# One product per query tile with the block maxima, ahead of the products with neighbouring keys

## The chip, the cores and the metric

One core of a Trainium2 chip runs the whole program in one launch. The metric is device time in microseconds, the median over runs. Engines are named as the profile names them: PE is TensorE's matmul stream, PEld its weight loads (one instruction stream issues both), DVE is VectorE, ACT is ScalarE, POOL is GpSimd, SP issues most DMAs.

## What is computed

Attention over 4 batches, 8 heads, 768 positions and 64 features per head, then a feed-forward layer. Each query sees two kinds of keys: the neighbouring positions (fewer than 16 away) and 24 block keys, each the maximum of 32 keys in a row, feature by feature. One softmax runs over both.

```python
k_sum = k.reshape(B, H, nb, block, D).max(axis=3)          # block 32: nb = 24
v_sum = v.reshape(B, H, nb, block, D).mean(axis=3)
scores_l = scale * np.matmul(q, k.transpose(0, 1, 3, 2))   # kept where |i - j| < 16
scores_s = scale * np.einsum('bhsd,bhnd->bhsn', q, k_sum) + np.log(block)
a = softmax(concatenate([masked scores_l, scores_s], axis=-1))
attn = np.matmul(a, concatenate([v, v_sum], axis=2))
h = x @ w_in                                               # x: attn as 3072 x 512
out = (h - np.tanh(h)) @ w_out                             # 512 -> 2048 -> 512
```

## The kernel before

The 3072 rows are cut into 8 units `u` of 384 rows (`U`): half a batch each. A unit has 4 head pairs `p`; a head pair has two heads (`a`), and its 384 queries make three query tiles (`i`, `NT = 3`) of 128 rows, each of two halves of 64. The features of head 0 lie on partitions 0 to 63 and those of head 1 on partitions 64 to 127.

`scores` (L1000) makes all scores of one head pair as one task on PE; there are 8 x 4 = 32 such tasks, called score blocks here. For each tile the task first multiplies with the 24 block maxima of `top` (far products), then with the at most 94 neighbouring keys of each half (near products; 79 at an end of the sequence). Head `a` writes its own PSUM bank, `ss[a]`: `pS` and a second one (`pY0`, later `pT`). Half 0 goes to partitions 0 to 63 of the bank, half 1 to partitions 64 to 127. Queries are the stationary operand (64 features x 64 queries), keys move. All operands are 32-bit floats, and the profile shows two weight loads and two matmuls for each product (called passes here): 24 products, 48 passes in a block. In units 0 and 1 queries and keys come from `qf` and `kT` (tiles `q`, `kT`), in units 2 to 7 from `rawq0` and `raw` (tiles `rawq`, `raw`).

Behind a block comes `softmax` (L1023): DVE takes the sum with a mask and its minimum for each tile and head, ACT the exponential, DVE the sums and the scaling. Then the probabilities are turned (`p turn`: on PE in units 0 and 1, by DVE and DMA later) and `values` multiplies them with `v`. Between these small tasks PE runs the feed-forward products (`pH` banks for the first layer, `pY` and others for the second).

Nothing is scheduled at run time. Each task is put on record by `do(kind, engine, cost, ...)`; `Plan.follow` (L337) emits all tasks in the order of a table written out by hand (`ORDER`) and uses the stated costs only to place up to some dozens of idle products (`keep_warm`, L1538: `ident` by `ident` into `pX`) in modelled gaps of the first 100 us. The `scores` task has a stated cost of 1.07 us before and after. `k turn` (L983, transposes of keys on PE) and `sum` (L878, block sums of `v`) are other PE tasks that are named below.

Of the kernel before, what the change touches and what calls it, by code (L numbers as in the profile page):

```python
# [535 lines left out]
def program(  # L536
# [12 lines left out]
    tensor, vector, scalar, gpsimd, sync = engines.values()  # L549
    B, H, S, D = q.shape  # L550
    DM, F = w_in.shape[0], w_in.shape[1]
    P = 128
    U = S // 2
    NT = U // P
# [3 lines left out]
    NB = S // 32  # L558
# [4 lines left out]
    WIN = 15  # L563
    NK = 64 + 2 * WIN
    N2 = NB + NK
# [20 lines left out]
    def do(kind, engine, cost, go, r=(), w=(), before=()):  # L586
        plan.add(kind, {engine: cost}, go, r, w, before)
# [16 lines left out]
    def bank(base, tag):  # L604
        plan.banks.add(base)
        if tag == "pX":
            made_by[base] = lambda: px_bank
            plan.ring(tag, 1, base)
            return base
        return buf(base, tag, [P, 512], bufs=2 if tag == "pH" else 1, pool=pp)  # L610

    def at(base):
        if base not in made:
            made[base] = made_by[base]()
        return made[base]
# [374 lines left out]
    def tops(b, p):  # L990
        base = ("top", b, p // PG)
        if base not in made_by:
            buf(base, f"top{p // PG}", [P, PG * NB])
        return base, p % PG
# [5 lines left out]
    def scores(u, p, tags):  # L1000
        ss, b, t0 = [bank(("s", u, p, a), tags[a]) for a in range(2)], u // 2, U * (u % 2)
        top, m = tops(b, p)
        if u < WHOLE:
            q_all, k_all = lambda: at(("qf",))[:, p % 2], lambda: at(("kT",))[:, p]
            r = [(("qf",), p % 2)] + [(x, n) for x, n in [(("kT",), (p, 0)), (("kT",), (p, 1)), (top, (m, 0)), (top, (m, 1))]]
        else:
            (q_all, qr), (k_all, kr) = block_q[u, p], block_k[b, p]
            r = [*qr, *kr, (top, m)]

        def go():  # L1010
            for i in range(NT):
                for near in range(2):
                    for a in range(2):
                        for half in range(2):
                            rows, x = slice(64 * a, 64 * a + 64), P * i + 64 * half
                            first = t0 + x - WIN
                            lo, hi = max(first, 0), min(first + NK, S)
                            w = k_all()[rows, lo:hi] if near else at(top)[rows, NB * m:NB * (m + 1)]
                            c = N2 * i + (NB + lo - first if near else 0)
                            tensor.matmul(at(ss[a])[64 * half:64 * half + 64, c:c + (hi - lo if near else NB)], q_all()[rows, x:x + 64], w, start=True, stop=True)  # L1020
        do("scores", PE, 1.07, go, r=r, w=[(s, 0) for s in ss])

    def softmax(u, p):  # L1023
# [402 lines left out]
    def moe_slot(m):  # L1426
        if PAIRS and FIRST <= m < NM:
            kk, n = divmod(m - FIRST, 4)
            pair, k = divmod(kk, HALF_F)
            return PAIRS[pair][n in (1, 2)], 2 * k + (n > 1)  # L1430
        return divmod(m, NF) if 0 <= m < NM else None

    def moe_at(j):

        return j if not PAIRS or j < FIRST else -1 if j < FIRST + GAP else j - GAP
# [12 lines left out]
    for j in range(NS + LAG + 3 + (GAP if PAIRS else 0)):  # L1448
        m, m1, m2 = (moe_slot(moe_at(j - LAG - n)) for n in range(3))
        early = j < NP * SLOTS  # L1450
        s0 = slot(j)
        if s0 is not None:
            u, p, i = s0
# [46 lines left out]
        if s0 is not None and not early:  # L1500
            u, p, i = s0
# [78 lines left out]
```

## Time and profile before

| | |
|---|---|
| median of 3 runs | 643.25 us (643.18 to 645.22) |
| the profiled execution | 641.7 us |
| its span, first to last instruction | 640.0 us |
| PE busy | 624.0 us, 97% |
| PEld busy | 532.0 us, 83% |
| DVE, ACT, POOL busy | 486.6, 422.6, 172.5 us |
| mean granted clock of PE | 0.995 |

The span is the profiled execution less 1.7 us around it. Durations in the profile come from that one execution. A matmul's record includes the time that its result takes to come through the array, so records of consecutive matmuls overlap, and a busy share of PE near 100% doesn't by itself say that it is fed without pause; distances between starts do. `64*128 64x24` in a row says that the stationary operand has 64 partitions and 128 columns and that 24 columns move.

### The profile page before, as it was taken

What the parts mean: (1) busy time and instruction counts of PE and PEld (TensorE: products, weight loads), DVE (VectorE), ACT (ScalarE), POOL (GpSimd) and SP (SyncE); (2) the same over time, 40 slices, a digit from 0 to 9 for tenths busy, and PEclk for the clock granted to TensorE, in tenths of its full rate; (3) what the DMA queues carried; (4) which work ended last, traced back from release to release, by engine and by line L of the source; (5) the groups of instructions that cost most, each with busy time, mean ns of one, the idle gap of its engine ahead of it and who ended that gap; (6) DMA issues with size and microseconds to landing.
All of it is one profiled execution on the core that took longest, in us unless ns stands there. A gap on an engine that the chain in (4) does not pass through costs nothing.

```text
span 640.0 us, 14660 instructions
## 1 busy us (share of the span) xinstructions
PE 624.0 (97%) x5163; PEld 532.0 (83%) x5163; DVE 486.6 (76%) x1349; ACT 422.6 (66%) x1270; POOL 172.5 (27%) x191
## 2 busy tenths in 40 slices
PE   6989999999999999999999999999999999999996
PEld 5877666688888888888888889988898889989995
DVE  3989999998797787567785788685659878677662
ACT  3979788678767777656767556555557754554545
POOL 2130003134313331130313104235351043315330
PEclk9989999999999999999999999999999999999998
DMA  8867886856687787877875641000000100000002
GB/s 297 199 197 225 226 231 191 182 116 185 162 165 161 186 228 167 186 174 160 236 198 165 192 132 55 0 2 1 0 2 1 65 35 1 1 1 1 2 0 102
DMA packets 159765, 77.27 MB, mean 121 GB/s; under 512 B 121704, under 2 KB 148552, under 8 KB 159688
## 3 DMA queue, kind: packets, MB, share of 16 engines
q1 hardware_dynamic: 159416, 76.09, 46.0%
q8 instruction: 42, 0.69, 0.5%
q14 instruction: 35, 0.29, 0.1%
q10 hardware_dynamic: 272, 0.20, 0.1%
HBM read 58.12 MB, written 17.84 MB: 119 GB/s over the span
## 4 chain that ended last, share of the span: by engine, by line
PE 85%; DVE 6%; DMA 4%; ACT 2%; SPq 1%; issue 1%; POOL 1%; DVEq 0%; POOLq 0%; ACTq 0%
PE pH L233 37%; PE pY L233 30%; PE pS L233 6%; PE pT L233 6%; PE pX L233 6%; DVE raw L233 2%; DMA raw<-in_moe_w_out_dram 1%; DVE tmp L233 1%; DVE prob L233 1%; SPq L233 1%; DMA xl<-in_k_dram 1%; DMA tmp<-in_v_dram 1%; DMA raw<-in_moe_w_in_dram 1%; DVE wf L233 1%; POOL xf L233 1%
## 5 line engine op out<-in xcount | busy, mean ns | idle before, releaser
L233 PE MATMUL pH<-xh,w 128*128 128x384 f32 x608 | 155.9, 346 | 0.0
L233 PE MATMUL pY<-wf,gh 128*128 128x512 f32 x321 | 133.9, 454 | 0.2 <-DVE gh L233 0.2
L233 ACT ACTIVATE prob<-prob,stats 128x118 f32<-128x118 f32 x298 | 109.4, 385 | 35.3 <-DVE stats L233 33.7
L233 PEld LDWEIGHTS pH<-xh,w 128*128 128x128 f32 x608 | 109.0, 188 | 9.2 <-issue 3.1
L233 POOL TENSOR_TENSOR gl<-gu,gh 128x384 fp32r<-128x384 f32 x45 | 46.9, 1041 | 134.1 <-ACT gh L233 71.7
L233 POOL TENSOR_TENSOR gu<-gu,gt 128x384 f32<-128x384 f32 x49 | 51.3, 1048 | 105.8 <-ACT gu L233 60.5
L233 PEld LDWEIGHTS pY<-wf,gh 128*128 128x128 f32 x321 | 59.4, 188 | 19.4 <-issue 10.8
L233 ACT ACTIVATE gu<-gu 128x384 f32<-128x384 f32 x128 | 65.7, 517 | 1.1
L233 ACT ACTIVATE gh<-gu 128x384 fp32r<-128x384 f32 x71 | 36.8, 520 | 42.3 <-PE pY L233 16.7
L233 PE MATMUL pH<-xl,w 128*128 128x384 f32 x192 | 64.6, 336 | 0.0
L233 ACT ACTIVATE gu<-tmp 128x384 f32<-128x384 f32 x64 | 33.2, 518 | 37.2 <-DVE gl L233 19.4
L233 DVE TENSOR_TENSOR gl<-gu,gh 128x384 fp32r<-128x384 f32 x67 | 41.1, 613 | 13.0 <-ACT gh L233 9.3
L233 DVE TENSOR_TENSOR gu<-gu,gt 128x384 f32<-128x384 f32 x63 | 35.5, 567 | 8.7 <-ACT gu L233 8.5
L233 ACT ACTIVATE gt<-pH 128x384 f32<-128x384 f32 x64 | 30.7, 482 | 15.8 <-PE pH L233 15.6
L233 ACT ACTIVATE gu<-pH 128x384 f32<-128x384 f32 x64 | 30.9, 482 | 14.3 <-PE pH L233 9.4
L233 ACT ACTIVATE gt<-tmp 128x384 f32<-128x384 f32 x64 | 32.4, 512 | 11.9 <-DVE tmp L233 7.9
L233 ACT ACTIVATION_READ_ACCUMULATOR prob<-prob,stats 128x1 f32 x192 | 36.6, 190 | 0.0
L233 PE MATMUL pY<-kT,gh 128*128 128x512 f32 x90 | 36.5, 406 | 0.0
L233 PEld LDWEIGHTS pH<-xl,w 128*128 128x128 f32 x192 | 36.0, 187 | 0.0
L233 PE MATMUL pY<-kT,gl 128*128 128x512 f32 x90 | 35.4, 394 | 0.0
L233 POOL TENSOR_TENSOR xf<-xf 128x256 f32<-128x256 f32 x25 | 19.5, 781 | 56.1 <-DVE xf L233 55.0
L233 DVE CUSTOM_DVE_ANT_0 prob<-pS,mask 128x118 f32<-128x118 f32 x96 | 25.6, 275 | 11.6 <-PE pT L233 10.2
(306 smaller groups left out, 1627.9 us busy)
## 6 DMA issues: line engine op xcount, KB each, us to landing
place<-turned SPq DMA_DIRECT2D x96, 96.0 KB
probT<-place SPq DMA_DIRECT2D x24, 384.0 KB
raw<-in_moe_w_in_dram SPq DMA_DIRECT2D x16, 512.0 KB
raw<-in_moe_w_out_dram SPq DMA_DIRECT2D x16, 512.0 KB
vw<-in_v_dram SPq DMA_DIRECT2D x80, 96.0 KB
rawq<-in_q_dram SPq DMA_DIRECT2D x96, 48.0 KB
tmp<-in_v_dram SPq DMA_DIRECT2D x24, 192.0 KB
raw<-in_k_dram SPq DMA_DIRECT2D x48, 96.0 KB
```

The lines of the kernel that those rows point to most:

```text
L233: return lambda *args, **kwargs: self._tc.keep_in_program_order(op(*args, **kwargs))
```

## The change

In `scores` the far products come out of the tile loop: a first loop over the three tiles and two heads makes one far product each, with all 128 queries of the tile as stationary operand, and writes both halves of the bank at once. The near products follow in a loop of their own, in the order in which they stood before. A block has 6 far and 12 near products after the change in place of 12 and 12. The task's reads, writes, stated cost and place in the order stay.

```diff
         def go():
             for i in range(NT):
-                for near in range(2):
-                    for a in range(2):
-                        for half in range(2):
-                            rows, x = slice(64 * a, 64 * a + 64), P * i + 64 * half
-                            first = t0 + x - WIN
-                            lo, hi = max(first, 0), min(first + NK, S)
-                            w = k_all()[rows, lo:hi] if near else at(top)[rows, NB * m:NB * (m + 1)]
-                            c = N2 * i + (NB + lo - first if near else 0)
-                            tensor.matmul(at(ss[a])[64 * half:64 * half + 64, c:c + (hi - lo if near else NB)], q_all()[rows, x:x + 64], w, start=True, stop=True)
+                for a in range(2):
+                    rows = slice(64 * a, 64 * a + 64)
+                    tensor.matmul(at(ss[a])[:, N2 * i:N2 * i + NB], q_all()[rows, P * i:P * i + P], at(top)[rows, NB * m:NB * (m + 1)], start=True, stop=True)
+            for i in range(NT):
+                for a in range(2):
+                    for half in range(2):
+                        rows, x = slice(64 * a, 64 * a + 64), P * i + 64 * half
+                        first = t0 + x - WIN
+                        lo, hi = max(first, 0), min(first + NK, S)
+                        c = N2 * i + NB + lo - first
+                        tensor.matmul(at(ss[a])[64 * half:64 * half + 64, c:c + hi - lo], q_all()[rows, x:x + 64], k_all()[rows, lo:hi], start=True, stop=True)
         do("scores", PE, 1.07, go, r=r, w=[(s, 0) for s in ss])
```

## Rows read from the trace of the kernel before

**Rows 1.** The page: busy us of each engine, share of the span, instructions.

```profile
PE 624.0 (97%) x5163; PEld 532.0 (83%) x5163; DVE 486.6 (76%) x1349; ACT 422.6 (66%) x1270; POOL 172.5 (27%) x191
```

**Rows 2.** A group of matmuls by shape: far products; busy us, mean ns.

```profile
L233 PE MATMUL pS<-top,rawq 64*64 64x24 f32 x288 | 19.6, 206 | 0.4 <-DVE rawq L233 0.4
```

**Rows 3.** Stretch 125 to 347: length, busy PE, PEld, DVE, ACT, POOL, granted clock, DMA.

```profile
125.00:347.00 222.00, 221.44 (x2509) 191.44 (x2509) 170.96 (x617) 156.05 (x568) 59.36 (x59) 1.00 0.74 176
```

**Rows 4.** Waits of PE: us in total, times, longest us.

```profile
PE pT L233 <- DVE prob L233: 1.6, 1, 1.6
...
PE pS L233 <- DVE rawq L233: 0.4, 1, 0.4
```

**Rows 5.** Timeline of weight loads, one score block: start us, duration us.

```profile
143.12 0.14 PEld L233 LDWEIGHTS pS<-top,rawq 64*64 64x64 f32 x2 [0.25 <-issue]
143.14 0.14 PEld L233 LDWEIGHTS pT<-top,rawq 64*64 64x64 f32 x2
143.18 0.14 PEld L233 LDWEIGHTS pS<-top,rawq 64*64 64x64 f32 x2
...
143.23 0.14 PEld L233 LDWEIGHTS pS<-raw,rawq 64*64 64x64 f32 x2
...
144.12 0.19 PEld L233 LDWEIGHTS pY<-kT,gh 128*128 128x128 f32 x1
144.23 0.19 PEld L233 LDWEIGHTS pY<-wl,gh 128*128 128x128 f32 x1
```

**Rows 6.** Timeline of matmuls in the same block.

```profile
143.43 0.18 PE L233 MATMUL pS<-top,rawq 64*64 64x24 f32 x1
...
143.63 0.24 PE L233 MATMUL pS<-raw,rawq 64*64 64x94 f32 x1
...
143.71 0.18 PE L233 MATMUL pS<-top,rawq 64*64 64x24 f32 x1
...
143.95 0.24 PE L233 MATMUL pT<-raw,rawq 64*64 64x94 f32 x1
```

**Rows 7.** Timeline of weight loads of a `p turn` (transposes, 64 partitions, 118 columns).

```profile
63.67 0.13 PEld L233 LDWEIGHTS pT<-ident,prob 64*118 64x118 f32 x1 [0.76 <-ACT gt L233]
63.67 0.13 PEld L233 LDWEIGHTS pS<-ident,prob 64*118 64x118 f32 x1
63.73 0.14 PEld L233 LDWEIGHTS pT<-ident,prob 64*118 64x118 f32 x1
```

**Rows 8.** Groups of weight loads by shape: busy us, mean ns of one.

```profile
L233 PEld LDWEIGHTS pH<-xh,w 128*128 128x128 f32 x608 | 109.0, 188 | 9.2 <-issue 3.1 <-ACT gu L233 0.3 <-ACT w L233 0.2
...
L233 PEld LDWEIGHTS pT<-top,rawq 64*64 64x64 f32 x288 | 15.8, 132 | 0.2 <-DVE qa L233 0.2
...
L233 PEld LDWEIGHTS pT<-probT,vw 118*64 118x64 f32 x288 | 9.4, 137 | 4.2 <-issue 3.1 <-PE pY L233 1.1
```

**Rows 9.** Instructions of the tile `probT`, PE: ns min/median/max, first and last start.

```profile
L233 PE MATMUL pY<-probT,vw x48: 222/222/271, 31.0 to 45.0; 118*64 118x64 f32 x48
```

**Rows 10.** Timeline of matmuls: the end of `values` and what follows.

```profile
31.48 0.46 PE L233 MATMUL pY<-probT,vw 118*64 118x64 f32 x10
31.87 0.38 PE L233 MATMUL pX<-ident 128*128 128x128 f32 x1
```

**Rows 11.** Timeline of matmuls inside a `k turn` (transposes).

```profile
30.53 0.23 PE L233 MATMUL pT<-ident,xl 64*128 64x64 f32 x1
30.54 0.27 PE L233 MATMUL pH<-ident,xl 64*64 64x64 f32 x2
```

**Rows 12.** Timeline of matmuls: the starts of the third and the fourth block.

```profile
27.94 0.24 PE L233 MATMUL pS<-top,q 64*64 64x24 f32 x2
...
32.66 0.24 PE L233 MATMUL pS<-top,q 64*64 64x24 f32 x2
```

**Rows 13.** The chain that ended last, 28 to 38 us: start us, us, what.

```profile
30.56 3.68 DMA raw<-in_moe_w_out_dram
...
37.72 0.24 PE pT L233
```

## The prediction

> **What bounds the kernel.** I read the page first: PE is busy for 97% of the span [rows 1]. Then one long stretch. A block has 12 far passes in each bank, so the 288 that bank `pS` shows from `rawq` are 24 of the 32 blocks [rows 2], those of units 2 to 7; they lie between 125 and 347 us, where PE is busy for 221.44 of 222.00 us at a granted clock of 1.00, the 2.4 GHz level [rows 3]. Records of matmuls overlap, so I looked third at the waits: of those that PE has behind score blocks the longest are 1.6 and 0.4 us [rows 4]. PE sets the time: what a block gains or loses on PE, the kernel gains or loses, but for such waits. Last I took one block apart by its starts [rows 5, 6].
>
> A block holds PE from its first weight load at 143.12 to the first load of the next product at 144.12 [rows 5]: 1.00 us, 32 us in all 32 blocks. Four chains run side by side in it, one for each bank and partition half: at 143.12 and 143.14 four loads start, two for each bank. Within a chain a load of 64 columns follows the other after 0.055 us (143.12, 143.18, 143.23), so four loads take the time of one. A near pass is longer than that: from its start at 143.63 to the far pass behind it at 143.71 it streams for 0.08 us [rows 6]. By its 24 columns against 94 a far pass streams for 0.02. One tile is 0.28 us (143.43 to 143.71), and that adds up: two near streams of 0.08, and two loads of nearly 0.06 that nothing hides, those of the second far pass and the first near pass, since only 0.02 of streaming stands ahead of each. The loads of the second near pass and of the next tile's first far pass lie under near streams.
>
> So the block is 3 x 0.055 for the first two far loads and the first near load, 0.16 for its two near streams, 2 x 0.28 for two more tiles, 0.01 by which bank `pT` runs behind, and 0.09 from the last near stream's end (start 143.95, plus 0.08) to the next load at 144.12. That is 0.985, against 1.00 measured.
>
> **What the change does to it.** *Removed:* 6 of 24 products, 12 of 48 passes. They streamed for 0.02 each in four chains, and half of their loads lay under near streams.
>
> *Added:* columns. A far product now loads all 128 queries of a tile. Two chains are left, one for each bank, with 3 products of 2 passes each: 6 loads of 128 columns in a row. The trace before has no load of 64 partitions x 128 columns outside transposes, so I bound it from both sides. Low: in a `p turn` loads of 64 x 118 follow each other after 0.06 us [rows 7], but these are transposes. High: behind the block two loads of 128 x 128 start 0.11 apart, at 144.12 and 144.23, before anything streams [rows 5]. The groups choose between them: 128 x 128 takes 188 ns, 64 x 64 132 ns and 118 x 64 137 ns [rows 8], so outside transposes the columns decide and not the partitions. I take 0.11: 0.66 until the last far pass streams. Both banks' loads can go together, as they do in the `p turn` (63.67 and 63.67 [rows 7]); if they could not, the far part would take twice as long.
>
> *Moved:* the far products ahead of all near ones. Their loads lose their cover: before, one in two lay under a near stream; now each meets only the 0.02 of another far pass. And inside the block the stationary shape changes from 64 x 128 to 64 x 64. Where only the columns of the shape change outside transposes, at the end of `values`, a pause stands: the last record ends at 31.94 (31.48 plus 0.46), records of this shape last 222 ns [rows 9], so it started at 31.72, streamed its 64 columns for 0.05 and was through at 31.77; the next load starts at 31.87 [rows 10], 0.10 later, as at the end of the block (0.09). Against it speaks the `k turn`, where 64 x 128 gives way to 64 x 64 within 0.01 us [rows 11]. Bounds: 0, and 0.11, which is 0.09 and the far stream of 0.02 under which the near load could else lie. I take 0.11, since the `k turn` consists of transposes alone. The Trainium skill (TensorEngine Tiling, Key Properties) says that a change of tiling mode drains the engine: by that rule the block takes 1.405, without it 1.295. The trace agrees at `values` and not at the `k turn`.
>
> *The new block:* 0.66 for far loads, 0.02 the last far stream, 0.09 the change of shape, 0.055 the first near load, 6 x 0.08 for near streams whose other loads are hidden, 0.01 and 0.09 at the end: 1.405. Against 1.00 measured that is 0.405 more, against the 0.985 of the same reckoning 0.42. I take 0.41.
>
> *Nothing else moves.* The task keeps its reads, writes, place and cost, so no wait and no DMA is added or put behind another one, and the idle products stay as they are. Its consumer, the minimum on DVE, waits for the whole task before and after, so `softmax` starts 0.41 later, and so does all that stands behind the block on PE. What DVE and ACT have to do (486.6 and 422.6 us [rows 1]) stays.
>
> *The sum:* 32 x 0.41 = 13.1 us. Cover: the third and fourth block, at 27.94 and 32.66 [rows 12], lie beside a chain that comes from a weight DMA of 3.68 us at 30.56 through DVE to PE at 37.72 [rows 13], where PE waited 1.6 us [rows 4]; their 0.8 us are hidden there. The wait of 0.4 us, for a query tile that no block feeds, is eaten up by the blocks ahead of it. If that cover is gone, 1.2 us come back. I expect a span of 640.0 + 11.9 = 651.9 and a profiled execution of 653.6 against 641.7. The median of the runs shown, 643.25, lies 1.55 above the profiled execution; added to the median the sum gives 655.2.
>
> **Rivals.**
> 1. *No pause at the change of shape.* As in the `k turn` [rows 11] the first near load lies under the last far stream: 0.41 - 0.11 = 0.30 a block, 9.6 us, less 1.2 of cover: 651.7. For it: that one group. Against it: the end of `values` [rows 10].
> 2. *Loads as fast as in transposes.* At 0.06 each the far part is 0.36 in place of 0.66 [rows 7]: 0.11 a block, 3.5 us, less some 0.6: 646.2. If the pause is missing too, nothing is left of it: 643.3, no change. Against it: the groups of loads [rows 8].
> 3. *Passes set the pace, and the kernel gets faster.* If a block's 1.00 us were the price of 48 passes, 0.0208 each, 12 fewer would save 0.25 us, and 32 blocks 8.0 us: 635.3. It decides from the point where the distance between issued passes, and not a chain's own load, spaces the starts. Against it: four loads start within some 0.02 us, and then each chain waits until 0.055 is over [rows 5]. A rule that points this way stands in the Trainium skill (TensorEngine Tiling, Instruction Overhead): a matmul costs about 60 cycles however few columns move. My estimate from that page at 2.4 GHz is 25 ns for each of 12 passes, 9.6 us in 32 blocks, 633.7. The trace disagrees: starts lie less than 0.02 apart in the block.
> 4. *The two banks' loads take turns.* 12 x 0.11 in place of 6 x 0.11: 1.07 a block, 34.2 us less 1.2 of cover, 676. Against it: the `p turn` [rows 7].
>
> **How the numbers follow.** The forecast, 0.41 a block, has 0.66; no pause 0.15; fast loads 0.06, and with no pause too 0.03; faster by passes 0.06; loads in turns 0.04. A change of 0.3%, 1.9 us, is about what a measurement of this kernel can tell from none. Faster has 0.06, the same 0.03, slower 0.91. The range reaches from 650.0, below the case without a pause, to 658.0, which is 0.46 a block with nothing hidden; forecast and first rival hold 0.81 together. The forecast's own range is 653 to 658.
>
> **What would show it.** In the trace after: half as many weight loads from `top`, of the shape 64 x 128 and 188 ns long, 0.11 apart in each bank; 0.11 between the last far matmul's start and the first near load; blocks of 1.41 us; the same work of the stretch 125 to 347 us taking some 9 to 10 us more, still without long waits of PE. Loads 0.06 apart would show the second rival, a near load right behind the last far matmul's start the first, blocks below 1.00 us the third. The prediction is wrong if a block's length and the span don't go together, for PE would then have had slack that its waits don't show.

## The result and the profile after

The changed kernel takes 652.65 us (652.02 to 653.95) against 643.21 us (643.10 to 645.22) of the kernel before beside it: a ratio of 1.0142, 95% interval 1.0115 to 1.0168. It is slower. Run once more beside other runs of before, the ratio was 1.0183, 1.0155 to 1.0212 (654.25 us; the last experiment below). The profiled execution took 652.1 us with a span of 650.3, against 641.7 and 640.0.

The page after: busy time of each engine, which answers to [rows 1], and the chain of work that ended last, by engine:

```profile
PE 635.6 (98%) x4779; PEld 543.3 (84%) x4779; DVE 488.6 (75%) x1349; ACT 422.4 (65%) x1270; POOL 172.1 (26%) x191
...
PE 92%; DVE 4%; ACT 1%; DMA 1%; POOL 1%; issue 0%; SPq 0%; DVEq 0%; POOLq 0%; ACTq 0%
```

PE has 384 passes fewer (5163 to 4779: 12 in each of 32 blocks) and is busy for 11.6 us more. DVE and ACT have the same instructions and the same busy time within 2 us. The chain is PE nearly throughout. Now one block, the same as in [rows 5] and [rows 6], which stands 1.71 us later in this execution. First its weight loads:

```profile
144.83 0.18 PEld L233 LDWEIGHTS pS<-top,rawq 64*128 64x128 f32 x1 [0.24 <-issue]
144.84 0.18 PEld L233 LDWEIGHTS pT<-top,rawq 64*128 64x128 f32 x1
144.94 0.19 PEld L233 LDWEIGHTS pS<-top,rawq 64*128 64x128 f32 x1
...
145.38 0.19 PEld L233 LDWEIGHTS pS<-top,rawq 64*128 64x128 f32 x1
...
145.61 0.14 PEld L233 LDWEIGHTS pS<-raw,rawq 64*64 64x64 f32 x2
...
146.26 0.19 PEld L233 LDWEIGHTS pY<-kT,gh 128*128 128x128 f32 x1
```

Then its matmuls:

```profile
145.41 0.27 PE L233 MATMUL pS<-top,rawq 64*128 64x24 f32 x1
...
145.62 0.30 PE L233 MATMUL pS<-raw,rawq 64*64 64x79 f32 x2
...
146.09 0.24 PE L233 MATMUL pT<-raw,rawq 64*64 64x94 f32 x1
```

What to see: the loads of 64 x 128 are 0.11 apart in each bank (144.83, 144.94; five distances make 0.55, to 145.38), and the two banks load at the same time, 0.01 apart. At that distance the last of them is through at 145.49 and its 24 columns, 0.02 of streaming, at 145.51; the first near load starts at 145.61: a pause of 0.10. The near part takes 0.48 from there to the last matmul's start, and the next product's load follows at 146.26. The block lasts 1.43 us in place of 1.00. All 24 blocks of units 2 to 7 last 1.42 to 1.43; a group of loads by shape shows the price of one, which answers to the 132 ns in [rows 8]:

```profile
L233 PEld LDWEIGHTS pS<-top,rawq 64*128 64x128 f32 x144 | 17.8, 187 | 8.5 <-issue 6.8 <-PE pY L233 1.1 <-DVE prob L233 0.6
```

Last the stretch from the start of the ninth block to the end of the 32nd, in both kernels (length, busy PE, PEld, DVE, ACT, POOL, granted clock, DMA share, GB/s). Before:

```profile
134.75:345.64 210.89, 210.32 (x2460) 182.76 (x2460) 160.15 (x592) 149.78 (x552) 57.73 (x57) 1.00 0.75 178
```

After:

```profile
136.09:356.22 220.13, 220.13 (x2172) 191.83 (x2171) 162.04 (x592) 150.21 (x553) 57.55 (x58) 1.00 0.72 171
```

The same work takes 9.24 us more; 24 blocks are longer by 10.37 (0.432 each). The missing 1.1 us lie nearly all at one place, the block that waits for its query tile in the kernel before [rows 4]. Its lines there (weight loads, then the matmul that waits):

```profile
320.80 0.20 PEld L233 LDWEIGHTS pS<-top,rawq 64*64 64x64 f32 x4 [0.84 <-DVE rawq L233]
321.25 0.14 PEld L233 LDWEIGHTS pT<-top,rawq 64*64 64x64 f32 x2 [0.25 <-DVE qa L233]
...
322.22 0.30 PEld L233 LDWEIGHTS pH<-xh,w 128*128 128x128 f32 x2
```

```profile
320.81 0.30 PE L233 MATMUL pS<-top,rawq 64*64 64x24 f32 x4 [0.42 <-DVE rawq L233]
```

PE waited 0.42 ahead of this block, and then bank `pT` could start only at 321.25, 0.45 behind `pS`, so that the block lasted 1.42 in place of 0.99. Only 0.14 of this counts as idle time of PE, since the records of the other bank cover the rest. In the changed kernel both are gone, and the same block lasts 1.42 with its wide loads: from the start of the block ahead of it to the start of the block behind it the changed kernel takes 0.22 us less than before, though two longer blocks, 0.86, lie in between.

### The profile page after: what moved, and what is told of

Same layout as the page of the kernel before. It is cut to its first block, busy times and chain, and to the rows that moved or that the text cites. A ratio compares the mean times of both kernels' runs of the same rounds, so it can differ in the third digit from the quotient of the medians.

```text
span 650.3 us, 13892 instructions
## 1 busy us (share of the span) xinstructions
PE 635.6 (98%) x4779; PEld 543.3 (84%) x4779; DVE 488.6 (75%) x1349; ACT 422.4 (65%) x1270; POOL 172.1 (26%) x191
## 4 chain that ended last, share of the span: by engine, by line
PE 92%; DVE 4%; ACT 1%; DMA 1%; POOL 1%; issue 0%; SPq 0%; DVEq 0%; POOLq 0%; ACTq 0%
PE pH L233 39%; PE pY L233 33%; PE pS L233 9%; PE pX L233 6%; PE pT L233 6%; DVE prob L233 1%; DMA xl<-in_k_dram 1%; ACT prob L233 1%; DVE raw L233 1%; POOL xf L233 0%; DVE tmp L233 0%; DMA out_dram<-xf 0%; DVE top L233 0%; DVE vw L233 0%; DVE vsum L233 0%
```

## The experiments

**The order alone.** Far products ahead of the near ones, but with 64 queries each as before:

```diff
+            for i in range(NT):
+                for a in range(2):
+                    for half in range(2):
+                        rows, x = slice(64 * a, 64 * a + 64), P * i + 64 * half
+                        tensor.matmul(at(ss[a])[64 * half:64 * half + 64, N2 * i:N2 * i + NB], q_all()[rows, x:x + 64], at(top)[rows, NB * m:NB * (m + 1)], start=True, stop=True)
             for i in range(NT):
...
```

> The order alone: all 12 far products of 64 queries stand ahead of all near ones, nothing is merged, and the stationary shape stays 64 x 64 through the block. My theory (the loss comes from wider loads and one change of shape, not from the order): six far loads of 0.055 us, the first near load 0.055, six near streams of 0.08, 0.01 and 0.09 at the end make 0.965 by the reckoning that gave 0.985 for the kernel before, so a block stays within 0.03 of 0.99 to 1.00 and the time within 1 us of 643.2. Rival (the far loads lose the near streams as their cover, and that is the loss): half of the far passes lose some 0.05 each in four chains, a block of 1.15 and about 646 us.

Measured: 641.22 us against 642.96, 0.9966 (0.9943 to 0.9989). Weight loads of the same block:

```profile
146.43 0.14 PEld L233 LDWEIGHTS pS<-top,rawq 64*64 64x64 f32 x2 [0.36 <-issue]
...
146.48 0.14 PEld L233 LDWEIGHTS pS<-top,rawq 64*64 64x64 f32 x2
...
146.77 0.14 PEld L233 LDWEIGHTS pS<-raw,rawq 64*64 64x64 f32 x2
...
147.42 0.19 PEld L233 LDWEIGHTS pY<-kT,gh 128*128 128x128 f32 x1
```

The block is as long as before, 0.99 us: six far loads and a near one follow each other, the near one 0.34 behind the first (146.43 to 146.77), and the other near loads lie under near streams. Losing the near streams as a cover costs nothing, because in the old order as many loads stood open. The first near load follows the last far one at the usual distance, so passing from far to near products makes no pause as long as the shape stays. The rival falls. The time came out lower than the block explains, so the kernel was run again:

> The kernel of e1 once more, in more rounds: it came out at 0.9966 [0.9943, 0.9989] of before though its score blocks have the length of before. Theory (the length of a block decides, the order inside it nothing): within 0.3% of before, the interval includes 1. Rival (far products ahead help, by a way not seen): again 0.995 to 0.998, the interval below 1.

Measured: 642.19 us against 642.22, 1.0001 (0.9976 to 1.0027). The order makes no difference that can be seen; the interval of the first comparison, which left out 1, did not hold up.

**The merge alone.** The wide far products in the tile loop, so that the stationary shape changes five times in a block:

```diff
             for i in range(NT):
+                for a in range(2):
+                    rows = slice(64 * a, 64 * a + 64)
+                    tensor.matmul(at(ss[a])[:, N2 * i:N2 * i + NB], q_all()[rows, P * i:P * i + P], at(top)[rows, NB * m:NB * (m + 1)], start=True, stop=True)
...
```

> The merge alone: a far product of 128 queries for each tile and head, left in the tile loop, so that the stationary shape changes five times inside a block and not once. My theory (each change of shape empties PE, 0.09 us from the last stream to the next load): a tile takes 0.22 for two wide loads, 0.02 stream, 0.09 pause, 0.055 load, 0.16 near streams, 0.09 pause; three make a block of 1.9 us, 0.9 more than before, 29 us in 32 blocks, less some 3 of cover: about 669 us. Rival (no pause; loads lie under streams of the other shape): a tile of some 0.36, a block of 1.1 to 1.2 us, 646 to 649 us.

Measured: 669.25 us, one execution, where the theory put it. Its loads, one of each kind:

```profile
148.73 0.18 PEld L233 LDWEIGHTS pS<-top,rawq 64*128 64x128 f32 x1 [0.25 <-issue]
...
149.07 0.14 PEld L233 LDWEIGHTS pS<-raw,rawq 64*64 64x64 f32 x2
...
149.39 0.18 PEld L233 LDWEIGHTS pS<-top,rawq 64*128 64x128 f32 x1
...
150.70 0.19 PEld L233 LDWEIGHTS pY<-kT,gh 128*128 128x128 f32 x1
```

A tile takes 0.66 (148.73 to 149.39), a block 1.97. Against the changed kernel that is 0.54 for four more changes of shape, 0.135 each: the pause of 0.10, and loads behind it that nothing covers. The rival, without a pause, falls. The Trainium skill (TensorEngine Tiling, Key Properties) says that a changed tiling mode drains the engine. The trace agrees in both directions of the change: 0.10 from the last far stream to the first near load, and some 0.09 from the last near stream to the next tile's wide load.

**One change of shape and a third of the wide loads.** Only the first tile's far products are merged, all stand ahead:

```diff
+            for a in range(2):
+                rows = slice(64 * a, 64 * a + 64)
+                tensor.matmul(at(ss[a])[:, :NB], q_all()[rows, :P], at(top)[rows, NB * m:NB * (m + 1)], start=True, stop=True)
+            for i in range(1, NT):
+                for a in range(2):
+                    for half in range(2):
...
```

> One change of shape as in the changed kernel, but a third of its wide loads: the first tile's far products have 128 queries, those of the other two tiles 64, all ahead of the near ones. Theory (two causes that add up: 0.055 more for each wide load, 0.11 for the change of shape): 0.22 wide loads, 0.02 stream, 0.09 pause, 4 x 0.055 for the narrow far loads, 0.055 the first near load, 0.48 near streams, 0.10 at the end: a block of 1.19 to 1.21 us. Rival A (wide loads alone make the loss of 0.43): 1.14 us. Rival B (the change of shape alone): 1.42 us. The time is read with less care: 32 x 0.2 = 6 over before, less cover, 646 to 649 us.

Measured: 650.38 us, one execution; its loads:

```profile
151.13 0.18 PEld L233 LDWEIGHTS pS<-top,rawq 64*128 64x128 f32 x1 [0.36 <-issue]
...
151.24 0.19 PEld L233 LDWEIGHTS pS<-top,rawq 64*128 64x128 f32 x1
...
151.47 0.14 PEld L233 LDWEIGHTS pS<-top,rawq 64*64 64x64 f32 x2
...
152.35 0.19 PEld L233 LDWEIGHTS pY<-kT,gh 128*128 128x128 f32 x1
```

The block lasts 1.22 us (1.21 to 1.22 in all others of units 2 to 7 but two, the ninth and the one that waits for its query tile), between both rivals and where two causes that add up put it. From 0.995 with no wide load to 1.21: 0.215, which is two loads that are 0.055 longer and a pause of 0.10. From there to the changed kernel's 1.43: 0.22, four more wide loads of 0.055. The time itself came out above the range that was expected; this execution has waits of PE that the block doesn't explain, 1.0 us at 101.7 and 0.7 at 265.0, both for `gh` from DVE.

**PE time alone.** The old products in the old order, and two idle products behind each block:

```diff
+            for _ in range(2):
+                keep_warm()
```

> The kernel before, with two idle products of 128 x 128 by 128 columns behind each score block: four passes of 0.11 us, 0.44 us of PE time, about what the change adds to a block, with the old products in the old order and nothing wider. Theory (the change costs what it holds PE longer, and only that): as slow as the changed kernel, 9 to 10 over before, 652 to 653.5 us. Rival (a part of the loss comes from scores that are ready later, or from DMA that the wide products disturb): clearly less, below 650 us.

Measured: 651.9 us, 1.0150 (1.0116 to 1.0183). Timeline of matmuls and of weight loads behind one block:

```profile
150.88 0.71 PE L233 MATMUL pX<-ident 128*128 128x128 f32 x4
151.35 0.48 PE L233 MATMUL pY<-kT,gh 128*128 128x512 f32 x1
```

```profile
150.88 0.52 PEld L233 LDWEIGHTS pX<-ident 128*128 128x128 f32 x4
151.32 0.19 PEld L233 LDWEIGHTS pY<-kT,gh 128*128 128x128 f32 x1
```

Counted from load to load, as the blocks are, the four idle passes hold PE for 0.44 a block (150.88 to 151.32), about what the change adds. The profiled spans are alike, 650.2 us and 650.3 of the changed kernel's first profile, both without a fall to half clock (the 1.2 GHz level) before 640 us. So a kernel with no wide product, no change of shape inside the block and scores ready as early as before is as slow as the changed one. What the change costs is PE time, and the rival, which wanted less than 650 us, falls. The medians leave room for a small part besides: beside the same runs of before the changed kernel had a median 2.4 us higher (654.25, the last experiment), though the two intervals overlap.

**Parts of the kernel.** The change in units 2 to 7 alone, and in units 0 and 1 alone, by a condition in front of `do`; `go_wide` is the changed `go`, `go_split` the old one, and `WHOLE` is 2. The second kernel has `u < WHOLE`:

```diff
...
+        go = go_wide if u >= WHOLE else go_split
```

> The change in units 2 to 7 alone, 24 of the 32 blocks. My theory (behind 125 us PE has next to no slack, and nearly all of the price shows): 24 x 0.43 = 10.4, less 0.6 for the wait at 320 us: 9.8 over before, about 653 us, as much as the whole change. Rival (the cover lies evenly over the kernel, so that a block costs 9.4 / 32 = 0.29 wherever it stands): 7.1 over before, 650.3 us.

> The change in units 0 and 1 alone, 8 of the 32 blocks. My theory (here PE waits for loads and for DVE, and a longer block takes the place of a wait): of 8 x 0.43 = 3.5 us some 1 shows or less, 643.2 to 644.3 us. Rival (evenly spread cover): 8 x 0.29 = 2.4 over before, 645.6 us. If the half clock after 39 us, which the profile of the changed kernel lacks, is kept away by the change, the mean granted clock of these runs lies at 0.998 and not at 0.995 in most of them.

Measured: units 2 to 7 651.19 us, 1.0110 (1.0065 to 1.0154), that is 7.1 us with an interval of 4.2 to 9.9, which doesn't tell the theory from its rival. The profile does. From the start of the ninth block to the end of the 32nd it has

```profile
134.13:354.26 220.13, 220.13 (x2172) 191.84 (x2172) 161.54 (x592) 150.12 (x553) 57.81 (x58) 1.00 0.72 171
```

which is 9.24 us more than before, the same as in the changed kernel: 0.385 for each of the 24 blocks, and not 0.29. Units 0 and 1 646.21 us, 1.0046 (1.0023 to 1.0069), 1.5 to 4.4 us: the theory, 1 us or less, falls here, and the rival's 2.4 lies inside. Of the 3.5 us by which eight blocks are longer most shows, and the mean granted clock was 0.994 to 0.999 and not mostly 0.998. In the profile the ninth block starts 2.66 us later than in before (137.41 against 134.75), with one stretch of half clock in each of the two executions; that is 0.33 a block against 0.385 behind, an estimate, since two such stretches need not cost the same (see the last experiment). This profile has another thing, waits of PE for DMA that lie in units 2 to 7, where this kernel is as before:

```profile
PE pT L233 <- DMA vw<-in_v_dram: 2.1, 1, 2.1
...
PE pX L233 <- DMA probT<-place: 0.9, 1, 0.9
```

**The changed kernel again.**

> The changed kernel once more, in more rounds, beside the same runs of before as e5 and e7. Theory: 9 to 11 over before, ratio 1.014 to 1.017; its sum with units 2 to 7 alone (1.011) and units 0 and 1 alone (1.0046) then agrees. Rival (the two parts give each other cover): below 1.012.

Measured: 654.25 us, 1.0183 (1.0155 to 1.0212), span 653.8 in the profiled execution; above the range of the theory and still further from the rival. It lies 3.5 us over the first profile of the same kernel, and 2.9 of that are there before the ninth block (139.00 against 136.09). A window of before, with the granted clock as the third number from the end:

```profile
36.00:47.00 11.00, 8.23 (x96) 7.34 (x96) 8.51 (x37) 8.14 (x26) 1.63 (x1) 0.84 0.55 145
```

Of the changed kernel, first profile:

```profile
36.00:47.00 11.00, 8.57 (x108) 7.65 (x107) 9.33 (x46) 9.20 (x25) 2.18 (x2) 1.00 0.63 173
```

Of the changed kernel, second profile:

```profile
10.00:36.00 26.00, 24.30 (x343) 20.00 (x341) 20.27 (x89) 19.45 (x63) 5.29 (x4) 0.93 0.78 223
36.00:50.00 14.00, 11.51 (x138) 10.35 (x137) 11.23 (x48) 9.83 (x28) 3.49 (x3) 0.88 0.67 198
```

Half clock, the 1.2 GHz level, was granted for one stretch of 3.41 us in this part of the profile of before (at 39.2), for none in the first profile of the changed kernel and for two in the second (18.1 and 45.4); where PE is at work throughout, each costs up to half its length, 1.7 us. By the distances between blocks the two in the second profile cost 1.6 each (against the first profile); the one of before cost 1.05 (against the order alone, whose first profile has none). Without such falls the spans are 638.3 to 638.9, 650.3 and 650.4 to 650.6. An estimate from these: at equal clock the change costs 11.3 to 12.3 us.

## Why the prediction was right

*PE sets the time.* Shown: idle passes of about the same length do the same.

*The wide loads.* 0.11 apart and 187 ns long, as taken from loads of 128 x 128; the lower bound from transposes didn't hold. Both banks load together, as in the `p turn`. The second and the fourth rival fall.

*The change of shape.* 0.10, taken as 0.09 (0.10 at `values`, 0.09 at the end of the block). The `k turn` was the wrong row for it, and the first rival falls; why its transposes show no pause stays open. The sign that the prediction named for this step was wrong: it expected 0.11 from the last far matmul's recorded start to the first near load, and 0.20 stand there (145.41 to 145.61). The record starts while its load still runs and is 0.27 long, where one behind a load of 64 columns took 0.18 [rows 6]; the pause has to be counted from the load.

*The block.* 1.43, predicted as 1.405 and, with the price of 0.41, as 1.41: 0.432 more in place of 0.41. Of the 0.025 over the sum 0.01 is the pause; the rest lies behind the first near load.

*The moved products.* Shown as nothing by the order alone. The prediction told the lost cover as if it were a price of its own, but its sum never had a term for it: both orders leave the same number of loads open.

*Passes set the pace.* 12 passes fewer gain nothing: the block of 36 passes is the longer one, and that of 48 is as long in the new order as in the old. The third rival falls. The Trainium skill (TensorEngine Tiling, Instruction Overhead) gives a matmul an overhead of about 60 cycles; an estimate from that at the 2.4 GHz level is 25 ns, or 1.2 us for 48 passes one behind the other. The trace disagrees where four chains run side by side: the 48 passes take 0.99 us. Whether the overhead holds within one chain these rows don't decide.

*The cover.* Predicted 1.2, of it 0.8 in units 0 and 1 and 0.4 behind. At equal clock 13.8 (32 x 0.432; the first block, which in one profile ran partly at half clock, with its first loads 0.22 apart, is counted as the others) less 11.3 to 12.3 leaves 1.5 to 2.5, and it lies in part where the prediction had none. Behind, it is 1.1 in place of 0.4, since the prediction went by PE's waits and so left out the late start of bank `pT` at 321.25. In units 0 and 1 the predicted wait did shrink, from 1.63 to 0.99 in both profiles of the changed kernel, but the next wait of PE grew. That one, 1.15 us before, also stands behind score blocks, and the prediction passed over it when it called 1.6 and 0.4 the longest. Before:

```profile
37.72 0.24 PE L233 MATMUL pT<-ident,prob 64*118 64x64 f32 x1 [1.63 <-DVE prob L233]
...
43.68 0.71 PE L233 MATMUL pX<-ident 128*128 128x128 f32 x4 [1.15 <-DVE vsum L233]
```

After, first profile; in the second the same waits are 0.99 and 1.51:

```profile
38.84 0.24 PE L233 MATMUL pT<-ident,prob 64*118 64x64 f32 x1 [0.99 <-DVE prob L233]
...
43.95 0.71 PE L233 MATMUL pX<-ident 128*128 128x128 f32 x4 [1.30 <-DVE vsum L233]
```

A further part lies between the starts of the sixth and the eighth block: 38.35 us before, 38.07 with the order alone, 38.56 after, though two longer blocks add 0.86. The larger block and the larger cover cancel: with the one stretch of half clock that before had (1.05 to 1.7), the first profile's span is 651.3 to 652.0, and 651.9 was predicted. That the sum comes out so close is luck; the block's price is shown, the cover was mis-sized.

*The median.* 652.65 and 654.25 against 655.2; the first lies in the stated range from 650.0, and just under the forecast's own, 653 to 658. The change was added to the median of before, as if every execution had the waits and the clock of the profiled one. The profiled executions differ by stretches of half clock and by waits for DMA; before ranged from 639.89 to 646.92 over the later runs. How often which of them falls into an execution was not measured, since only profiled ones show it; so why the first ratio lies lower than the second stays open beyond that.

## What to carry to other kernels

Count weight loads by the columns of a chain, not by instructions: here, merging two loads of 64 columns that ran side by side into one of 128 halved the instructions and doubled the time, with next to no stream over them. No run here puts such a merged load under a longer stream. Before merging small products on part of the array, look for two loads of the target shape that start one behind the other with nothing streaming, and for the pause where the stationary shape changes; both prices could be bounded from the trace before. A wait of one bank alone hardly shows in PE's idle time; it is read from the distance between the two banks' first loads. A gain or loss of some us in one profile is compared only after the stretches of half clock have been counted in both.

## What was not expected of the hardware

In two profiles of one and the same kernel the granted clock fell twice for 3.41 us in the first 50 us or not at all. Of all ten profiles four had no such fall in this part, five had one and one had two, each for 3.41 us. In the execution where it did not fall PE had waited 1.0 us up to 38.8 and 1.3 up to 43.9; where it fell, 1.0 up to 40.1 and 1.5 up to 45.4, and the second fall came at 45.4. In that of before it fell at 39.2, after a wait of 1.6 up to 37.7.

In units 2 to 7 PE can come to wait for DMA: the kernel changed only in units 0 and 1 waited there for 2.1 and 0.9 us in its profile, waits that neither profile of the whole change has. What sets them off stays open.
